# A new instruction order for agent attention with a SiLU MLP, and an empty instruction as token between banks

## Chip, cores and metric

The kernel runs on one NeuronCore of a Trainium2 chip. The metric is the device time of one execution in microseconds (us). TensorE is called PE here (PEld is its weight load), VectorE DVE, ScalarE ACT, GpSimd POOL, and SyncE, which only issues DMAs, SP.

## What is computed

Two batches of 12480 tokens with 128 channels, 49 agents in each batch, then a dense MLP with 2048 hidden units on all 24960 tokens. Inputs are float32 (the two weights are float64).

```python
def _attn_ref(q, k, v, agents):
    scale = 1.0 / np.sqrt(q.shape[-1])
    def sm(a, b):
        s = scale * (a @ b.transpose(0, 2, 1))
        s = s - s.max(-1, keepdims=True)
        e = np.exp(s)
        return e / (e.sum(-1, keepdims=True) + 1e-09)
    agent_v = sm(agents, k) @ v
    return (sm(q, agents) @ agent_v).astype(np.float32)

def _moe_ref(x, w_in, w_out):
    h = x @ w_in
    g = h * (1.0 / (1.0 + np.exp(-h)))
    return (g @ w_out).astype(np.float32)
```

## The kernel before, in words

Tokens go in 13 tiles of 960 per batch, 26 in all. For a batch, all tiles of k and v are folded into the 49 x 128 matrix `agent_v` (running maximum, exponentials, transposes, products); that matrix times `w_in` gives the folded weight A2 of the batch, held as two float16 parts `A2h` and `A2l`. For a q tile the softmax over the agents is made and turned by a DMA into `pT`. The MLP then runs on the tile in 16 steps of 128 hidden units, 416 steps in all.

- **front** (`front`, L610): six matmuls make the hidden block `h` of a step.
- **gate** (`gate`, L622, ACT): SiLU into half of a tile `g`, which holds two steps, a pair.
- **hi half** (`split`, L636 on ACT or L638 on DVE, as the string `HI` says) and **lo half** (L642, DVE) split `g` into the float16 tile `hl` (one of its six buffers bears the name `vx`).
- **back** (`back`, L664): twelve matmuls of a step add into two PSUM banks `o0` and `o1`. The halves of the PE array swap banks in the middle of every four backs. So that the third back of four does not write before the second has ended, the second is followed by a token on POOL (L670), a memset of one element that waits for the last matmuls of the second back; the first matmuls of the third back wait for that memset.
- **out_part** (L687 DVE, L689 ACT) scales a finished tile into an output tile `os`, of which there are two, and **out_store** (L697, SP) stores it.

The q tiles from the third on have a path of their own, two tiles at a time: `q_absmax` (L338, DVE) takes the largest magnitude of each tile into a small tile `mx2`; `q_total` (L342, PE) sums it into a PSUM tile `x`; `q_scales` (L192, L349, L352, DVE) makes from it the scales `sk`, `ik` and two tiles `es`; `split_khl` (L756 ACT, L759 DVE) splits the q tile and frees its load buffer (`kq`, five of them, shared with k); `q_exp` (L569, ACT) uses `es`; `q_norm`, `q_parts` (DVE) and `q_turn` (L588, DMA) make `pT`. The small tiles are rings: two `mx2`, two `sk`, three `ik`, six `es`, so a writer waits for the reader of the tile before last, and so on. PSUM tiles `x` are a ring of two, which a_mm (L542, the product that makes A2) uses too.

No engine chooses its work at run time. Four strings in `PLAN`, one letter per job, fix the order of the jobs on SP, PE (P), ACT (A) and DVE (D); `issue` takes the next letter of each engine when what `job` was given as `deps`, `after` and buffers (`take`, `give`) has been issued, and `in_order` ties every instruction to the one before it on its engine. At run time an instruction waits for what it reads and for the buffer it overwrites, whatever stands in `deps` or `after`; an instruction that waits holds up all that stands behind it on its engine. The strings come from a planner outside the file, which is not shown here.

Of the kernel before, what the change touches and what calls it, by code (L numbers as in the profile page):

```python
# [48 lines left out]
PLAN = {
    "S": (  # L50
        "kakkkqvkawkwkvkkkkkkvvvvwvvqwvvvvvkkkqtkqvvtqqtvkvvkkvkqoovktqvtktokkvqqvootvovkqqqtotqqovqttqqotqqt"
        "qoootqoqtqotqqottottoootttootoototoo"),
    "P": (
        "WkkwkwwwukQwwkwwwwwwwwwwwwkttwwwwwtvktkvkktktkwwwwkvvv1ttww2ttvv3vwwQtwwwwwwwvttvvvvk4ua56aakffafmff"
        "fkbffbfbfbbffbffbfbffbbfbbttbffbfbbffqqfbbffbfbbbffbtkvvmfbffbbfbfbfbfbffbbkvkfbfbffbbffbfbqqfbfbfbf"
        "bffbbbbfbttbffbbffbffbffbftvkkmbfbbffbbffbbbffbvvkffbfbffbbffbbfbbffbqqbfbfbffbbffbbfbfttfbffbbfbfvt"
        "mbfbfbfbkvvkkfbfbbffbffbffbbffbbffbbfbfqqbffbbffbffbkfbfbfbbbbffbbttfbfbtmfbbfbfbffvvvt1ffbbbfbffbfb"
        "fbbfbbffbffbffb2qmbfbb3vfbbffb4qfbfbffbbfbffbbffbbfbfbffbbfbbfbffb6aaffbffbbbfbbffbbffbqqfbfbfbfbfbf"
        "bbfbfbfbbfbbfmaafbfbfbffbbffbffbbbffbffbfbbfbfbbffbfmqffbqmbfbfbfbfbbffbbfqmfbffbfbbfbffbffbbfbfqqbb"
        "bfbfbfbfbfbfbbffbfbbffbfbfbfbfbfbqmfbffbfbbfbfbbqmbffbffbffbbffbbbffbffbbbffbfbfbffbbfbfbqqffbfbfbbf"  # L60
        "fbbffbbffbbffbbffbfbffbbffbfbffbbbfbfbffbqqffbbfbfbfbbfbbffbffbffbbbffbffbfbfbbffbffbbbffbbffbbffbbf"
        "bbffbffbbbffbbbffbfbbfqffbfbfbbbffbffbfbbffbffbbbbffbbffbfbfbffbfbfbffbffbbbffbbbfbffbbffbbfbffbfbbf"
        "bffbfbfbfbffbbbfbbffbbfbffbfbffbfbfbbffbfbfbbbfbbffbffbfbfbffbbffbbffbbffbfbbbfbffbffbbfbbffbfbfbfbb"
        "bfbbbbbb"),
    "A": (
        "xxcectttxxtcxcttxttxfccttetccttskawaakggagggigggiggiggwggghgkgxghggigotggiggggeegikgighggiggiggihokg"
        "gggiggkggggiggggxeggioggggggtggkggegggigkhhggigggoggkgiggiggxggggggeggtgoggeigggiikhgghkggiggggggkig"
        "gogigigggggggiggiggxkeegoggtiggxggigghgigghgggiiggogggggfggegiggiggigghgggoggegggggiggigggagghagoggi"
        "giggiggggeegggiggohgaghggiggaggggiggggiggigogggihgggigghgiggigghggiggggoggieeegghigggghggiggigoggigg"
        "giggiggiggggeeeggggoggigiggghggihggggggiggoiggggiggigggghggigggggogghgggiiggiggggggeeeggogggghggiggg"  # L70
        "gggiggiggggoggggegggiggigiggiggogggggegggggggiggiggoggggggggggiggiggigggoggigggeggggggggiggoggiggggg"
        "ggiggggggoggggggggggggiggggggogggigggggigo"),
    "D": (
        "xr12sxr5xnr1657xr8xprxrdx6dr73845d90d67s5An86d7dd8BCE2FDyamaamGwiajHyjpcijjjijwiylrijjtiljomjsjisjnp"
        "mtdjcjiljjydjnopjliyjdjijiyssjjirjminjptojimjijitdjijyincjjilydjjiopjlydrjijisjjijisjijiomtjmdjtnncp"
        "jdydijyjjijijjoylrpljjijisjsmjjimjyotnrnijijctjdmddpj3ljijtmpjjoijij49sicj0dnlApjijBjsjijiojijiEnijj"
        "jpFmjlijimjolmaajmjssjiGijnjijmjicpojijnjilHjaijjpijlamjojiscjljmjsimjcjjisljjicojlijnpsjnjiijjljspo"
        "jmmjijjmsljjmcijinjiojpnjjijiljcjijlsipjojnpjijjjsijiljjijiojijnjsljjijpijinjoijiijjjijinjsjjijoiiji"
        "pjjlsjnpjjjoijiijjijiijpjnjjiojijijijsijpjjjiojjijijijijnpijjoinjjijijjipjijijoijijijijijjijijoijijj"
        "ijjijo"),  # L80
# [945 lines left out]
```

## Time and profile before

| | us |
|---|---|
| median of three runs | 909.35 |
| lowest and highest run | 905.48, 909.81 |
| the profiled execution's own time | 909.31 |
| its span, first to last instruction | 907.5 |
| PE busy in the span | 873.9 |
| DVE busy, ACT busy | 813.0, 728.4 |

The span leaves out 1.8 us of the execution's time. Matmul ends are modelled, so a busy PE is not always PE at its peak. In the timeline a bracket at a row's end gives how long the engine stood idle before the row and what ended that.

### The profile page before, as it was taken

How to read it: one execution, taken by the hardware profiler on the slowest of the kernel's cores; microseconds unless marked ns; L12 is line 12 of the kernel's file. 1: busy time of each engine (PE TensorE's matmuls, PEld its weight loads, DVE VectorE, ACT ScalarE, POOL GpSimd, SP SyncE). 2: the span in 40 equal slices, each digit the busy share in tenths (PEclk: the TensorE clock that was granted, in tenths of full speed). 3: DMA queues.
4: the chain of work that ended last, by engine and by line, in shares of the span. 5: the costliest groups of instructions: out<-in, count | busy, mean ns of one | idle time of the engine just before them, and what ended most of it. 6: DMA issues, size and time to landing. Idle time of an engine off the chain costs nothing.

```text
span 907.5 us, 20159 instructions
## 1 busy us (share of the span) xinstructions
PE 873.9 (96%) x8879; PEld 443.4 (49%) x8879; DVE 813.0 (90%) x817; ACT 728.4 (80%) x704; POOL 24.5 (3%) x114
## 2 busy tenths in 40 slices
PE   7989999999999999999899799899999999999997
PEld 4645555545554555445345344454544444444443
DVE  4799989999999899998899688999999899799985
ACT  4579997788988989888689779788887977877563
POOL 1000000000000000000000000000000000000000
PEclk9999999999999999999899899999999999999999
DMA  9982074016014023030040112110010101101100
GB/s 346 389 266 56 1 196 134 15 43 186 23 35 144 22 81 87 2 78 2 11 122 23 46 45 67 35 35 13 2 56 23 25 1 56 35 2 35 34 23 22
DMA packets 43410, 63.89 MB, mean 70 GB/s; under 512 B 29475, under 2 KB 29731, under 8 KB 42811
## 3 DMA queue, kind: packets, MB, share of 16 engines
q1 hardware_dynamic: 43323, 62.61, 23.0%
q8 instruction: 69, 1.13, 0.5%
q14 instruction: 18, 0.15, 0.1%
HBM read 43.01 MB, written 12.78 MB: 61 GB/s over the span
## 4 chain that ended last, share of the span: by engine, by line
PE 82%; DVE 6%; ACT 3%; issue 1%; POOL 1%; DMA 1%; SPq 0%; POOLq 0%; DVEq 0%; ACTq 0%
PE o L664 52%; PE h L610 25%; DVE hl L642 3%; PE x L479 1%; DVE hl L638 1%; ACT g L622 1%; PE x L380 1%; POOL token L670 1%; PE x L463 1%; PE x L361 1%; DMA outT<-os 1%; PE x L362 1%; PE x L363 1%; PE x L542 0%; ACT hl L636 0%
## 5 line engine op out<-in xcount | busy, mean ns | idle before, releaser
L622 ACT ACTIVATE g<-h,sA 128x960 f32<-128x960 f32 x416 | 425.0, 1057 | 106.7 <-PE h L610 97.3
L642 DVE SCALAR_TENSOR_TENSOR hl<-g,tS,hl 128x1920 f16<-128x1920 f32 x173 | 380.7, 2213 | 21.5 <-ACT hl L636 19.1
L664 PE MATMUL o<-hl,woh 64*128 64x480 f16 x2768 | 383.9, 365 | 13.0 <-DVE os L687 6.6
L664 PEld LDWEIGHTS <-woh 64*128 64x128 f16 x3328 | 164.7, 94 | 189.8 <-issue 15.8
L610 PE MATMUL h<-pT,A2h 64*128 64x480 f16 x1664 | 238.9, 364 | 0.7 <-ACT g L622 0.6
L664 PE MATMUL o<-hl,wol 64*128 64x480 f16 x1384 | 198.7, 365 | 0.0
L610 PE MATMUL h<-pT,A2l 64*128 64x480 f16 x832 | 153.8, 364 | 0.0
L636 ACT ACTIVATE hl<-g,tS 128x1920 f16<-128x1920 f32 x76 | 143.7, 1894 | 1.4
L610 PEld LDWEIGHTS <-A2h 64*128 64x128 f16 x1664 | 83.0, 94 | 89.2 <-issue 10.7
L638 DVE TENSOR_SCALAR hl<-g,tS 128x1920 f16<-128x1920 f32 x97 | 117.6, 1213 | 9.5 <-ACT g L622 9.4
L664 PEld LDWEIGHTS <-wol 64*128 64x128 f16 x1664 | 83.1, 94 | 86.5 <-issue 1.4
L664 PE MATMUL o<-vx,woh 64*128 64x480 f16 x560 | 79.9, 363 | 1.3 <-DVE os L687 1.3
L642 DVE SCALAR_TENSOR_TENSOR vx<-g,tS,vx 128x1920 f16<-128x1920 f32 x35 | 77.4, 2212 | 1.3 <-PE o L664 0.5
L610 PEld LDWEIGHTS <-A2l 64*128 64x128 f16 x832 | 41.6, 94 | 43.2 <-issue 0.7
L670 POOL MEMSET token<- 1x1 f32 x104 | 21.9, 211 | 875.3 <-PE o L664 868.1
L664 PE MATMUL o<-vx,wol 64*128 64x480 f16 x280 | 39.9, 362 | 0.0
L689 ACT ACTIVATE os<-o,oS 128x480 f32<-128x480 f32 x26 | 17.2, 661 | 23.4 <-PE o L664 21.3
L687 DVE TENSOR_SCALAR os<-o,oS 128x480 f32<-128x480 f32 x26 | 18.6, 715 | 15.1 <-PE o L664 13.3
L338 DVE TENSOR_REDUCE mx<-q 128x1 bf16<-128x960 f32 x24 | 27.4, 1147 | 4.5 <-PE x L342 4.5
L638 DVE TENSOR_SCALAR vx<-g,tS 128x1920 f16<-128x1920 f32 x24 | 29.1, 1213 | 1.3 <-ACT g L622 1.3
L756 ACT ACTIVATE khl<-q,ik 128x960 f16<-128x960 f32 x24 | 26.1, 1090 | 4.8 <-DVE ik L349 4.8
L759 DVE SCALAR_TENSOR_TENSOR khl<-q,ik,khl 128x960 f16<-128x960 f32 x24 | 29.0, 1210 | 0.0
(171 smaller groups left out, 559.8 us busy)
## 6 DMA issues: line engine op xcount, KB each, us to landing
k<-kT SPq DMA_DIRECT2D x26, 480.0 KB, 8.1
q<-qT SPq DMA_DIRECT2D x26, 480.0 KB, 5.1
outT<-os SPq DMA_DIRECT2D x25, 480.0 KB, 3.1
vt<-vP SPq DMA_DIRECT2D x13, 480.0 KB, 7.7
vt<-vP SPq DMA_DIRECT2D x9, 512.0 KB, 8.4
...
```

Of the source, the lines that this page charges most:

```text
L338: V.tensor_reduce(st["mx", n][:, u:u + 1], tiles[key], axis=AX.X, op=ALU.max, apply_absolute_value=True)
L610: T.matmul(ps[:, u, :HT], w[wt][rs, fs], t[rs, x * HB:(x + 1) * HB, 0:CH], start=(n == 0), stop=(n == 2))
L622: A.activation(hid[s // 2][:, s % 2], hps.pop(s)[:, :, :HT], AF.Silu, scale=batch[b]["sA"][:, 0:1])
L636: A.activation(hid[p][1], g, AF.Copy, scale=t)
L638: V.tensor_scalar(hid[p][1], g, t, None, op0=ALU.mult)
L642: V.scalar_tensor_tensor(lo, g, t, hi, op0=ALU.mult, op1=ALU.subtract)
L664: mm = T.matmul(acc[u], wt[rs, j + x, :], g[rs, x, u, :], start=(a and x == 0 and n == 0), stop=(z and x == 1 and n == 2)).ins
L670: acc["told"] = G.memset(token, 0.0).ins
L687: V.tensor_scalar(o[:, 0:HT], last_acc[0], oS, None, op0=ALU.mult)
L689: A.activation(o[:, HT:ST], last_acc[1], AF.Copy, scale=oS)
L756: A.activation(t[:, 0, 0:ST], tiles[key], AF.Copy, scale=st[key, "inv"])
L759: V.scalar_tensor_tensor(l[:, 0:ST], tiles.pop(key), st.pop((key, "inv")), hi[:, 0:ST], op0=ALU.mult, op1=ALU.subtract)
```

## The change

The strings `HI` and all four of `PLAN` are new. In the job table some conditions move from `after` (issued before) to `deps` (a need), which is what the planner reads; for the program itself `issue` treats both alike. The conditions are the reuse of `mx2` (q_total of the pair four q tiles earlier), of `ik` and `es` (lo split and exponentials of six and five q tiles earlier), of the output tiles (the store two tiles earlier) and of the v buffers of batch 1 (each of the first four waits for the one product of batch 0 that read it, where all of them waited for the last). The token is `nop` where it was `memset`, and its tile is gone, so line numbers behind L598 are lower by one.

```diff
 HI = (
-    "DAADADDDDAADAADAAADADDADDADDDDDADADADADDDDDAAADADDAAADDAADDADAADAADDDADAADDDDDAADDAAADDDADDADDADAADA"
+    "DADAAADDDAAADDADAADDDDAAADAADADAAADDDDDAAAADDADDDAAADDDDADAADAADDDDAAADADADDADADDAAADDAADDADAAADADAD"
...
     "S": (
-        "kakkkqvkawkwkvkkkkkkvvvvwvvqwvvvvvkkkqtkqvvtqqtvkvvkkvkqoovktqvtktokkvqqvootvovkqqqtotqqovqttqqotqqt"
+        "kkakkwkkvqvkkkkwkkkvvwvvvvqwvvvvvakkktqqkqvkvtqovvvkktqqkktvkkqvktqovtkvqotovvqotvqqtvqoqtooqqtqoqto"
...
-    token = cp.tile([1, 1], F32, name="token")
...
         if r == 1:
-            acc["told"] = G.memset(token, 0.0).ins
+            acc["told"] = G.nop(nofuse=True).ins
             for mm in mms.values():
                 tc.add_manual_dep(acc["told"], mm.name, SYNC, reason="banks")
...
-            xs_.append(job("D", "m", q_absmax, key, n, u, deps=[l], after=xs_ + ([lows[n - 4][0]] if n - 4 in lows else [])))
+            xs_.append(job("D", "m", q_absmax, key, n, u, deps=[l] + ([lows[n - 4][0]] if n - 4 in lows else []), after=xs_))
         x = job("P", "m", q_total, n, deps=xs_, take=("x",))
-        sc = job("D", "c", q_scales, n, keys, deps=[x] + [ags[key[1]] for key in keys], give=("x",),
-                 after=[lows[n - 6][1], expd[n - 5]] if n - 6 in lows else [])
+        sc = job("D", "c", q_scales, n, keys, deps=[x] + [ags[key[1]] for key in keys] +
+                 ([lows[n - 6][1], expd[n - 5]] if n - 6 in lows else []), give=("x",))
...
-            l = job("S", "v", load, *key, take=("vt",), after=avl[-1:])
+            l = job("S", "v", load, *key, take=("vt",), deps=[avl[(12, 7, 8, 9)[i + u]]] if i + u < NV else [])
...
-            parts_ = [job("DA"[u], "o", out_part, k, u, deps=ready, after=stores[n - 2:n - 1] if n > 1 else [],
+            parts_ = [job("DA"[u], "o", out_part, k, u, deps=ready + (stores[n - 2:n - 1] if n > 1 else []),
```

Three places of the new order follow, each as it was and as it is.

**Place 1, reuse of `es`, batch 1, pairs around step 210 to 218.** ACT before (`L569` are the exponentials that read `es_5694` and `es_5696`; a number in `g` or `h` is the step):

```order
L622 ACTIVATE g214_6559<-h215_6560,sA1_4979 128x960
L689 ACTIVATE os_207_6581<-o1_192_6104,oS0_714 128x480
L622 ACTIVATE g216_6590<-h216_6583,sA1_4979 128x960
L622 ACTIVATE g216_6590<-h217_6591,sA1_4979 128x960
L636 ACTIVATE hl5_893<-g214_6559,tS1_4981 128x1920
L569 ACT_TABLE_LOAD
L569 ACTIVATE D_6156<-D_6156,es_5694 120x392
L569 ACTIVATE D_6288<-D_6288,es_5696 120x392
L569 ACTIVATE D_6462<-D_6462,es_6162 120x392
```

DVE before, where `es_6608` and `es_6610` take the places of `es_5694` and `es_5696`:

```order
L638 TENSOR_SCALAR hl4_892<-g212_6504,tS1_4981 128x1920
L192 TENSOR_SCALAR sk_6604<-x_6435 128x2
L349 RECIPROCAL ik_6606<-sk_6604 128x2
L352 TENSOR_SCALAR es_6608<-sk_6604,ags1_727 128x1
L352 TENSOR_SCALAR es_6610<-sk_6604,ags1_727 128x1
L687 TENSOR_SCALAR os_207_6581<-o0_192_6103,oS0_714 128x480
L642 SCALAR_TENSOR_TENSOR hl4_892<-g212_6504,tS1_4981,hl4_892 128x1920
```

The same on ACT now (the exponentials read `es_4677`, `es_5590` and `es_5592`):

```order
L621 ACTIVATE g216_6627<-h217_6674,sA1_4681 128x960
L569 ACT_TABLE_LOAD
L569 ACTIVATE D_6232<-D_6232,es_4677 120x392
L569 ACTIVATE D_6239<-D_6239,es_5590 120x392
L569 ACTIVATE D_6420<-D_6420,es_5592 120x392
L621 ACT_TABLE_LOAD
L621 ACTIVATE g218_6715<-h218_6708,sA1_4681 128x960
L621 ACTIVATE g218_6715<-h219_6772,sA1_4681 128x960
```

and on DVE now, where `es_6808` takes the place of `es_4677`:

```order
L641 SCALAR_TENSOR_TENSOR vx_112<-g216_6627,tS1_4683,vx_112 128x1920
L637 TENSOR_SCALAR hl1_113<-g218_6715,tS1_4683 128x1920
L192 TENSOR_SCALAR sk_6802<-x_6380 128x2
L349 RECIPROCAL ik_6804<-sk_6802 128x2
L352 TENSOR_SCALAR es_6806<-sk_6802,ags1_726 128x1
L352 TENSOR_SCALAR es_6808<-sk_6802,ags1_726 128x1
L641 SCALAR_TENSOR_TENSOR hl1_113<-g218_6715,tS1_4683,hl1_113 128x1920
```

Before, the DVE wrote `es` ahead of the lo half of pair 212, while the exponentials that it waits for stood behind the gates of pair 216. Now it writes `es` behind the hi half of pair 218, whose gates stand behind those exponentials on ACT.

**Place 2, reuse of `mx2`.** PE before (`x_5679` is q_total of `mx2_5131`, `x_5681` and `x_5702` are the first two a_mm of batch 1):

```order
L610 MATMUL h180_5671<-pT_5138,A2l0_710 128x480
L342 LDWEIGHTS ones12_94
L342 MATMUL x_5679<-mx2_5131,ones12_94 128x2
L542 MATMUL x_5681<-win_114,avT_100 128x512
L542 MATMUL x_5702<-win_114,avT_100 128x512
L610 LDWEIGHTS A2h0_709
```

DVE before, where `mx2_5686` takes the place of `mx2_5131`:

```order
L638 TENSOR_SCALAR hl3_891<-g174_5504,tS0_713 128x1920
L642 SCALAR_TENSOR_TENSOR hl3_891<-g174_5504,tS0_713,hl3_891 128x1920
L338 TENSOR_REDUCE mx2_5686<-q_1_5_5282 128x1
L642 SCALAR_TENSOR_TENSOR hl4_892<-g176_5568,tS0_713,hl4_892 128x1920
L638 TENSOR_SCALAR hl5_893<-g178_5611,tS0_713 128x1920
L192 TENSOR_SCALAR sk_5690<-x_5679 128x2
```

The same tile of q on DVE now, where `mx2_5168` takes the place of `mx2_3810`:

```order
L637 TENSOR_SCALAR hl2_835<-g160_5118,tS0_712 128x1920
L641 SCALAR_TENSOR_TENSOR hl1_113<-g158_5086,tS0_712,hl1_113 128x1920
L338 TENSOR_REDUCE mx2_5168<-q_1_5_5034 128x1
L551 SCALAR_TENSOR_TENSOR A2l1_4680<-x_4816,iA1_4682,A2h1_4679 128x512
L641 SCALAR_TENSOR_TENSOR hl2_835<-g160_5118,tS0_712,hl2_835 128x1920
```

and q_total of `mx2_3810` on PE now:

```order
L363 MATMUL x_4592<-agh0_255,khl1_106 128x49
L342 LDWEIGHTS ones12_94
L342 MATMUL x_4626<-mx2_3810,ones12_94 128x2
L609 LDWEIGHTS A2h0_708
L609 MATMUL h138_4628<-pT_3690,A2h0_708 128x480
```

Before, the reader stood on PE behind front 180, and the DVE wanted the tile just behind the lo half of pair 174. Now the reader stands ahead of front 138, and the DVE wants the tile behind the hi half of pair 160, which needs front 161.

**Place 3, the load queue ahead of the store of tile 9 (`os_159`).** SP before (`q_1_7` takes the load buffer that the split of `q_1_2` frees; on DVE that split stands four rows ahead of the write of `os_191`, which takes the place of `os_159`):

```order
L234 DMA q_1_6_5828<-qT 128x960
L588 DMA_TRANSPOSE pT_5830<-phl0_98 128x8x128
L234 DMA q_1_7_5956<-qT 128x960
L697 DMA outT<-os_159_5273 128x960
L697 DMA outT<-os_175_5684 128x960
```

and now (`q_1_6` takes the buffer that the split of `q_1_1` frees, on DVE 60 rows ahead of the write of `os_191`):

```order
L696 DMA outT<-os_143_4935 128x960
L234 DMA q_1_6_5371<-qT 128x960
L588 DMA_TRANSPOSE pT_5373<-phl1_99 128x8x128
L696 DMA outT<-os_159_5353 128x960
L588 DMA_TRANSPOSE pT_5817<-phl0_98 128x8x128
```

The store now stands behind a load that is freed much earlier.

## Rows read from the trace of the kernel before

**Rows 1.** The page: engines, busy us, share; then the chain that ended last.

```profile
PE 873.9 (96%) x8879; PEld 443.4 (49%) x8879; DVE 813.0 (90%) x817; ACT 728.4 (80%) x704; POOL 24.5 (3%) x114
...
PE 82%; DVE 6%; ACT 3%; issue 1%; POOL 1%; DMA 1%; SPq 0%; POOLq 0%; DVEq 0%; ACTq 0%
```

**Rows 2.** Stretches: length, then busy us of PE, PEld, DVE, ACT, POOL; clock; DMA.

```profile
0.00:60.00 60.00, 50.27 (x483) 32.99 (x485) 42.93 (x102) 30.36 (x52) 2.58 (x10) 1.00 0.99 366
...
100.00:425.00 325.00, 324.77 (x3375) 165.98 (x3373) 305.80 (x319) 287.07 (x276) 8.98 (x39) 1.00 0.27 73
425.00:575.00 150.00, 135.22 (x1372) 65.94 (x1370) 127.67 (x127) 117.68 (x107) 2.46 (x17) 0.94 0.17 48
```

**Rows 3.** Timeline at 431 to 436: start, us, engine, line, work, count [idle before].

```profile
431.18 0.18 PE L342 MATMUL x<-mx,ones 128*128 128x2 bf16 x1
...
431.22 1.10 PE L542 MATMUL x<-win,avT 128*128 128x512 f32 x2
431.40 1.16 DVE L338 TENSOR_REDUCE mx<-q 128x1 bf16<-128x960 f32 x1 [4.51 <-PE x L342]
...
435.93 2.07 PE L542 MATMUL x<-win,avT 128*128 128x512 f32 x2 [3.60 <-DVE sk L192]
```

**Rows 4.** Chain that ended last, before and after that wait: start, us, what.

```profile
427.61 0.61 PE h L610 x6
428.21 2.43 PE o L664 x24
...
438.00 1.31 PE h L610 x6
439.32 2.08 PE o L664 x12
```

**Rows 5.** Timeline of DVE, ACT and PE at 509 to 512, then the chain there.

```profile
510.14 0.21 DVE L352 TENSOR_SCALAR es<-sk,ags 128x1 f32<-128x1 f32 x1 [6.37 <-ACT D L569]
...
509.49 1.65 ACT L569 ACTIVATE D<-D,es 120x392 f32<-120x392 f32 x3
...
511.55 0.98 PE L664 MATMUL o<-hl,woh 64*128 64x480 f16 x4 [6.62 <-DVE os L687]
...
511.55 4.80 PE o L664 x24
```

**Rows 6.** Timeline of PE at 568 to 571, then the chain behind it.

```profile
568.79 0.58 PE L664 MATMUL o<-hl,woh 64*128 64x480 f16 x4 [1.33 <-DVE hl L638]
571.05 0.98 PE L664 MATMUL o<-hl,woh 64*128 64x480 f16 x4 [1.26 <-DVE hl L642]
...
572.03 2.28 PE h L610 x12
```

**Rows 7.** Timeline of DVE and PE at 464 to 471.

```profile
463.98 1.21 DVE L759 SCALAR_TENSOR_TENSOR khl<-q,ik,khl 128x960 f16<-128x960 f32 x1
...
470.52 0.72 DVE L687 TENSOR_SCALAR os<-o,oS 128x480 f32<-128x480 f32 x1 [1.49 <-DMA outT<-os]
...
471.29 0.58 PE L664 MATMUL o<-vx,woh 64*128 64x480 f16 x4 [1.34 <-DVE os L687]
```

**Rows 8.** PE's waits for the token; the token's durations; tokens over 150 ns; one place.

```profile
PE o L664 <- POOL token L670: 3.4, 7, 0.7
...
L670 POOL MEMSET token<- x104: 88/88/1130, 71.1 to 900.3; 1x1 f32 x104
...
147.15 1.13 POOL L670 MEMSET token<- 1x1 f32 x1 [7.81 <-PE o L664]
...
872.55 0.86 POOL L670 MEMSET token<- 1x1 f32 x1 [6.59 <-PE o L664]
...
531.05 1.22 DVE L638 TENSOR_SCALAR hl<-g,tS 128x1920 f16<-128x1920 f32 x1 [2.42 <-ACT g L622]
531.25 1.04 POOL L670 MEMSET token<- 1x1 f32 x1 [7.20 <-PE o L664]
...
532.36 0.58 PE L664 MATMUL o<-hl,woh 64*128 64x480 f16 x4 [0.62 <-POOL token L670]
```

More of the change, by code (lines that the diff above doesn't have):

```diff
@@ L45 @@
 HI = (
-    "DAADADDDDAADAADAAADADDADDADDDDDADADADADDDDDAAADADDAAADDAADDADAADAADDDADAADDDDDAADDAAADDDADDADDADAADA"
-    "ADAADADADADDAAADAAADDDAADDADDAADAADDADDDAAADDDDDDADDAADDDDAAAADDDDDDAADDDDDAAADADDDDDADADDADDDDDDDDA"
-    "DDDDADAD")
+    "DADAAADDDAAADDADAADDDDAAADAADADAAADDDDDAAAADDADDDAAADDDDADAADAADDDDAAADADADDADADDAAADDAADDADAAADADAD"
+    "ADADADDADDDAAADADADAAADDADDDDDDADDADAADAADADDDDDDDAADDADADAADDDDADDDDDDDDDADDDDDADDAADDAADDDDDADADAD"
+    "AADDADDD")
 PLAN = {
     "S": (
-        "kakkkqvkawkwkvkkkkkkvvvvwvvqwvvvvvkkkqtkqvvtqqtvkvvkkvkqoovktqvtktokkvqqvootvovkqqqtotqqovqttqqotqqt"
-        "qoootqoqtqotqqottottoootttootoototoo"),
+        "kkakkwkkvqvkkkkwkkkvvwvvvvqwvvvvvakkktqqkqvkvtqovvvkktqqkktvkkqvktqovtkvqotovvqotvqqtvqoqtooqqtqoqto"
+        "tqqqtoqtootqoqtototttooottotooottooo"),
@@ L53 @@
     "P": (
[L54 to L63, printed above, removed]
@@ L64 @@
-        "bfbbbbbb"),
-    "A": (
[L66 to L72, printed above, removed]
@@ L73 @@
-    "D": (
[L74 to L80, printed above, removed]
+        "WwwwwwwwwwwkkwwwwwwwwukkwwwkttkvQwwktkkwkvtwwwwwktktkvvwww1ttwt2vvv3vtQtwwwwwvtvvtvvww4ku5w6aaafaffk"
@@ new lines @@
+        "fffkmfbfbffbbfbfbfbbfbfbffbfbfbfbttbfqqbffvkfbfbmtbfbbfbfvkvkffbbbffbffbfbfbbfbffbfqqfbbkbttbmtfbffb"
+        "ffbbffbbffbbfbbffbfbffkvvkvqqffbbffbfbfbfbffbbbfbfbbfbfbfbbffbffbfbbbfttbfbffbfbbffbbmkvktffbbffvvkk"
+        "qffbffbffbbfbbffbfbfbfbbbfbfbbffbfbbftqfbfbfbtmfbbbfbffbffbfbfbbbbfbfbfftvvvt1fbfbfbffbfbfbfbf2qmfbb"
+        "b3vbfbfbfbfbfbffbbfbfbb4qmfbfbfbfbfbffbf6aaffbfbbfbffbffbbfbfbfbfbffbffbbbffbbbfbffbbqqffbfbfbbbbffb"
+        "ffbfbfmaabfbffbfbfbfbbffbqmfbffbbfbfbffbbbffbfbffbbbfbffbqqfbfbffbbfbfqmbfbfbffbbfbbfbbffbffbfqfbbfb"
@@ new lines @@
+        "bbbffbffbfbbffbbffbfbfbbfqmffbbfbbfbffbfbbfbmqfbffbbbffbfbbffbfbfbffbbbffbfbffbffbfbbfbbfbfbffbbffbb"
+        "fbfbffbbqqfbffbffbfbbfbfbfbffbfbfbbffbfbfbfbffbfbfbbbfbfbbffbfbfbbffbffbffbbbfbfbfbfbbfbfbfqqfbbffbf"
+        "bfbfbfbffbbbffbbffbbfbbffbffbfbffbbbffbbfbfbfbfbfbfbffbffbffbbfbbffbfbfbfbbffbffbbqffbbffbfbffbbfbff"
+        "bbbfbfbbbffbffbbfbfbbffbbffbbfbfbfbffbfbffbffbbffbfbfbbffbbfbbfbfbffbbfbfbffbfbfbbfbbffbfbfbbbfbffbf"
+        "fbbbfbbbbbb"),
+    "A": (
+        "xtccxtxexttxtcctxtxctfcttetccttskawaagaggkggigggigkgwggiiggghgghgxggtgigogikgiggeeghkgghgiggkggiggig"
+        "gogggxkteegggggighgigggigghgikggkioggggigggggeiggigiggoggggxeggggggtiggikhgkghiggkiggggoggiggggxeggg"
+        "kgigggioggigxegggggtgggigggghoiggiggggiggghgfieggggggoggiggiggigghgggigagggaigggoggigghggggiggeggigg"
+        "ioghggiggeeggggiggaigaggggigogghgiggiggggighgggiggigogghgiggghgiggggiegghggggogigeeeggggggiggiggiggo"
+        "ggghiggggihgggiggiggigoghggggigggggggggeegggoggiggggggigggggigigggoggiggigggigghggeegghggogggggggggi"
+        "gigggegggoigghggiggggiggigggggogggggggiggggggggggggoggeggggiggggggegggggoggigggeggiggiggggoggiggiggg"
+        "gggggggggiggogggigggigggggigiggoggggiggggggo"),
@@ new lines @@
+    "D": (
+        "xr152xrxr678sxrxr5nxrxr6d7358d4d9p6d07As5n86d7d1d8BCE2FDyGamaHamaijwjiyjcyjpwjjijirjlitljssojdmmjcji"
+        "ytjdnlpiyjjiyrjdjnjlopssiimmtjjcyijijjnjltjipjdydldyrojjijsjnisjnmjjjoijiipjpjmitjijjcdynpytjddlyjji"
+        "orjijjsijmijinyrjjlmmotjsjipjmijicjmijnjijtdoddtljpjijj34s9mcljijijd0iojiAjjBjncEpjsijFljimjjiojiajj"
+        "ijmlijijmajnGjojlspsjimjijncjjiajijaojijpHlnjscjijjplmijmjojsiljsijjsijjjlijiojnjpmijicjlijjsmjjonip"
+        "jljicmjsmjinjjjpnojijijsjijijpiijjlciojijljiijjjsnpijjjiojnjjijjipjiljiljoijijijisjnjnjipjipojjsijnj"
+        "ijpjjijijosijijijjijiljijijiojijijijjijinijjijopijsjiijnjjnpjijoijjjijijijijipjojijjijjijjjoijijjiji"
+        "jijo"),
@@ L922, in agent_attention_then_silu_mlp @@
             kept.append(x)
-            x = job("P", "v", lambda key: av_products(key, psum(C)), key, deps=[l, x], take=("x",), give=("vt", "eT"))
+            x = job("P", "v", lambda key: av_products(key, psum(C)), key, deps=[l, x], take=("x",), give=(("vt", l), ("eT", x)))
             y = job("D", "d", av_add, key, g, u == 0, deps=[x] + ([y] if y else [avend]), give=("x",))
@@ L946, in agent_attention_then_silu_mlp @@
             e = HI[p]
-            x = job(e, "i", split, p, 0, A if e == "A" else V, deps=gates[-2:] + [unit1[b]] + ([avl[NST - 1]] if p == 0 else []),
-                    after=his_[-1:] + ([ws[w, h] for w in ("in", "out") for h in range(NW)] if p == 2 else []), take=("hl",))
+            x = job(e, "i", split, p, 0, A if e == "A" else V, deps=gates[-2:] + [unit1[b]] + ([avl[NST - 2]] if p == 0 else []) +
+                    ([ws[w, h] for w in ("in", "out") for h in range(NW)] if p == 2 else []), after=his_[-1:], take=("hl",))
             his_.append(x)
```

## Prediction

> **What bounds the kernel now.** I read the page first. PE is busy 96% of the span, and the chain that ended last lies 82% on PE [rows 1]. DVE, at 90%, is close behind and is the engine on which a misplaced instruction hurts. Only less matmul work or fewer holes on PE can shorten such a kernel. The change keeps the matmuls: counted by letters, both orders have 416 fronts, 416 backs, 26 jobs each for scores of k, turns and products, 24 of q; only the warming matmuls grow, by six. So the question is where PE stands idle or slow.
>
> The second view cuts the span into stretches [rows 2]. From 100 to 425 us PE is busy 324.77 of 325 us: there is nothing to win there, and it shows that the order's plan of durations is good. From 425 to 575 us PE is busy 135.22 of 150 us, at a granted clock of 0.94. In the first 60 us it is busy 50.27 us, while the DMA engines are full (share 0.99, 366 GB/s). The holes are thus in the start and in one piece of 150 us in the middle.
>
> The third view is the timeline and the chain in that piece: four places, each a wait for a buffer that is overwritten.
>
> 1. *mx2.* At 431.40 the DVE has stood 4.51 us, until q_total (L342) on PE has read the small tile that absmax (L338) overwrites [rows 3]. Behind it on DVE stand a lo half, a hi half, then the scales that free the PSUM tile for the second a_mm; PE waits 3.60 us for it.
> 2. *es.* At 510.14 the DVE has stood 6.37 us until ACT has done the exponentials that read the old `es`; behind it stand the output write and the lo half of pair 212. PE waits 6.62 us [rows 5].
> 3. *es again.* At 568 PE waits 1.33 and then 1.26 us for the halves behind another such write [rows 6].
> 4. *os.* The store of tile 9 stands on SP behind a load that waits for the split at 463.98; the output write waits 1.49 us for that store, PE 1.34 us [rows 7].
>
> Idle is not the whole price. Behind the first wait a front takes 1.31 us where it took 0.61 before it, and twelve matmuls of a back 2.08 us, where 24 took 2.43 [rows 4]; that is the lower of the two clock levels (1.2 against 2.4 GHz), granted after PE had stood idle.
>
> **The change, part by part, against the profiled execution's own 909.31 us** (the median is 909.35, so nothing is to be shifted).
>
> *mx2 wait goes.* Idle 3.60. Slow matmuls: the a_mm pair 2.07 - 1.10 = 0.97 [rows 3], the front 1.31 - 0.61 = 0.70, the back 2.08 - 2.43/2 = 0.86 [rows 4]. Sum 6.1 us. In the new order (place 2) the reader stands ahead of front 138, the writer behind a hi half that needs front 161: 23 fronts later on PE, so the tile has been read whenever the DVE gets there. What is late next is nothing: the DVE then waits for the front, as in the stretch without holes.
>
> *First es wait goes.* Idle 6.62, and 24 matmuls in 4.80 us against 2.43: 2.37 [rows 5, 4]. Sum 9.0 us. Place 1 shows why it can't come back there: the hi half of pair 218 on DVE needs gates that stand on ACT behind the exponentials, so the write of `es` behind that half finds them done.
>
> *Second es wait goes.* 1.33 + 1.26 idle, and twelve matmuls of two fronts in 2.28 us against 2 x 0.61: 1.06 [rows 6, 4]. Sum 3.65 us.
>
> *os wait goes.* 1.34 us [rows 7]. In place 3 the store of tile 9 now stands behind a load whose buffer is freed 60 DVE rows ahead of the write that needs the store, where it was four.
>
> *Token.* Of 104 memsets 21 took over 150 ns (the first 1.13 us at 147.15, the last 0.86 us at 872.55), the median 88 ns; PE waited 3.4 us in 7 of them [rows 8]. At 531 the memset starts 0.20 us after a DVE hi half (L638) and ends with it, 532.29 against 532.27; each of the 21 ends so with an L638. The trace before has no empty instruction. Its bounds: no gain if it is held as the memset was, 3.4 us if it never is. I take 3.4, since it writes nothing that a DVE instruction could hold; even at 88 ns it would be hidden behind the front that stands between second and third back in nearly all cases. The Trainium skill ("SBUF — State Buffer", section "SBUF: two separate sides") says that VectorE and GpSimd share a port pair as an exclusive lock, so that one of the two blocks fully. By that rule an instruction without an SBUF operand is never held and the term is the full 3.4 us; without it, by the rows alone, the term could be 0 and the sum 889.2. This trace agrees for the memsets; no run here shows the empty instruction.
>
> *Start: 0.* The loads are issued in another order, but up to the last v load of batch 0 both orders hold the same 13 k, 13 v, 4 weight and 2 q loads, on full DMA engines, and the first front needs that last v. The agents of batch 1 go from the ninth load to the place right behind the last v; the DVE reads them ahead of the last sum for `agent_v`, but they are small and issued next to a tile of 480 KB that the same chain awaits. Bounds: two loads of 480 KB later at 366 GB/s is +2.6 us; filling all of PE's idle 60.00 - 50.27 is -9.7 us. I take 0, nearer to the first. The six warming matmuls lie in this idle time.
>
> *Hi halves.* Two of 208 go from DVE to ACT. ACT is busy 80%, so PE covers it; if it didn't, it would show as a PE wait for ACT.
>
> Sum: 909.31 - 6.1 - 9.0 - 3.65 - 1.34 - 3.4 = **885.8 us**.
>
> **Rivals.**
>
> *A new wait takes the place of the old ones.* The strings are new throughout, and DVE has only 325 - 305.8 = 19 us to spare in 325 [rows 2], so one instruction placed some us too early reaches PE, as the four did. For it: the old strings had four such places in 150 us. Against it: all four were buffers whose reuse the old job table gave as order alone, and the new one gives as a need; elsewhere the old strings had next to no holes. Price: one hole as large as the largest seen, 9.0 us: 894.8.
>
> *The start moves.* Another order of loads may let PE fill its idle time: half of 9.7 us gives 881, all of it 876. For it: PE and DVE both have holes there. Against it: the DMA engines are full and the last v bounds it.
>
> *The strings don't do what they say.* Nothing in the program's own waits has changed; were the four waits only moved, the sum would be the token's term alone, 906 to 909. The rows of places 1 to 3 speak against it.
>
> *Slower, by the token.* 104 times PE waits for a signal that goes through POOL. If the empty instruction takes longer than a memset does, every third back is late. With one front in between, a token of 1.04 us left PE idle 0.62 us [rows 8], so the cover is 0.42 us. In the new order 59 third backs have just one front in between (51 before). From 0.42 + 23.5/59 = 0.82 us on, the gain is gone; at the longest memset's 1.13 us the 59 cost 42 us: 928. Only the length of the slowest memsets speaks for it, and those are the held ones; the 88 ns speak against it.
>
> **How the numbers follow.** The forecast, 880 to 892, has 0.72. A new large hole has 0.14 (892 to 902). A start that gains over 6 us has 0.07 (below 880). Waits only moved: 0.04. Slower by the token: 0.03. The range leaves out most of the last three and the far end of the second, some 0.17 in all: 879.5 to 897. A measurement of this kernel tells about 0.5% from no change, 4.5 us; all of the first three cases are faster by more, 0.93; same 0.04, slower 0.03.
>
> **What would show it.** In the new profile: no DVE row of L338 or L352 with an idle of some us ended by PE or ACT, and no output write that waits for a DMA; a granted clock of 1.00 in every stretch of 425 to 575; PE's waits in the middle below 2 us together; tokens that never outlast 0.1 us, and no PE wait on POOL. The prediction is wrong if PE shows a new wait of over 4 us anywhere behind 100 us, if the first front (L610) starts over 3 us away from where it did, at 60 us (where the first stretch of [rows 2] ends), or if the backs wait for POOL.

## The result and the profile after

The changed kernel takes 880.71 us, median of four runs (880.28 to 881.33), against 908.36 (905.48 to 909.81) for the kernel before: a ratio of 0.97, 95% interval 0.9673 to 0.9727. The prediction was 885.8 us, its range 879.5 to 897. Direction and mechanism hold. The time is 5.1 us below the forecast; counted from the medians beside it, 27.7 us were won where the sum gave 23.5, 4.2 more, and 2.6 of that is a term that the sum had at zero, the start. The profiled execution took 880.8 us, its span is 878.7.

The page of the profile after, the lines of [rows 1]: busy us, share and instructions of each engine, then the chain that ended last.

```profile
PE 866.4 (99%) x8885; PEld 439.7 (50%) x8885; DVE 811.2 (92%) x815; ACT 730.1 (83%) x704; POOL 2.6 (0%) x10
...
PE 94%; DMA 2%; DVE 2%; ACT 1%; issue 0%; SPq 0%; ACTq 0%; POOLq 0%
```

PE's share of the chain went from 82% to 94%, DVE's from 6% to 2%. The stretches of [rows 2], with 60 to 100 us between them:

```profile
0.00:60.00 60.00, 53.10 (x497) 35.21 (x499) 44.06 (x105) 32.08 (x54) 2.57 (x10) 1.00 0.98 362
60.00:100.00 40.00, 39.33 (x407) 19.24 (x402) 39.04 (x38) 39.66 (x39) 0.00 (x0) 1.00 0.26 70
100.00:425.00 325.00, 325.00 (x3359) 164.69 (x3359) 308.10 (x326) 289.84 (x277) 0.00 (x0) 1.00 0.27 75
425.00:575.00 150.00, 149.97 (x1602) 74.01 (x1598) 145.66 (x138) 133.33 (x120) 0.00 (x0) 1.00 0.18 48
```

From 425 to 575 us PE is busy 149.97 of 150 us where it was 135.22, at a granted clock of 1.00 where it was 0.94. The first 60 us hold 53.10 us of PE work where they held 50.27, and that was not foreseen.

The groups of instructions by line, 100 to 700 us, for the three writes that waited on the reuse of a buffer: line, engine, operation, count, then busy us, mean ns of one, and the idle time of the engine just before them with what ended it. First before:

```profile
L338 DVE TENSOR_REDUCE mx<-q 128x1 bf16<-128x960 f32 x21 | 24.0, 1147 | 4.5 <-PE x L342 4.5
L687 DVE TENSOR_SCALAR os<-o,oS 128x480 f32<-128x480 f32 x18 | 12.9, 715 | 8.0 <-PE o L664 6.3 <-DMA outT<-os 1.5
L352 DVE TENSOR_SCALAR es<-sk,ags 128x1 f32<-128x1 f32 x22 | 3.7, 201 | 10.2 <-ACT D L569 10.2
```

and after:

```profile
L338 DVE TENSOR_REDUCE mx<-q 128x1 bf16<-128x960 f32 x22 | 25.0, 1147 | 0.0
L686 DVE TENSOR_SCALAR os<-o,oS 128x480 f32<-128x480 f32 x18 | 12.9, 714 | 1.7 <-PE o L663 1.5
L352 DVE TENSOR_SCALAR es<-sk,ags 128x1 f32<-128x1 f32 x22 | 3.5, 199 | 0.0
```

The instructions and their durations are the same; the idle time that PE's q_total (4.5 us), ACT's exponentials (10.2 us) and the store (1.5 us) ended is gone. What is left before `os` is the wait for the finished tile itself, which belongs to the work.

All waits of PE behind 62 us in the profile after (total us, times, longest):

```profile
PE h L609 <- ACT g L621: 0.6, 1, 0.6
PE o L663 <- DVE hl L641: 0.2, 1, 0.2
```

No wait on POOL stands here, where [rows 8] had 3.4 us in seven.

### The profile page after: what moved, and what is told of

It is laid out like the page before. It is cut to its first block, busy times and chain, and to the rows that moved or that the text cites. A ratio compares the mean times of both kernels' runs of the same rounds, so it can differ in the third digit from the quotient of the medians.

```text
span 878.7 us, 20055 instructions
## 1 busy us (share of the span) xinstructions
PE 866.4 (99%) x8885; PEld 439.7 (50%) x8885; DVE 811.2 (92%) x815; ACT 730.1 (83%) x704; POOL 2.6 (0%) x10
## 3 DMA queue, kind: packets, MB, share of 16 engines
q8 instruction: 69, 1.13, 0.5%
## 4 chain that ended last, share of the span: by engine, by line
PE 94%; DMA 2%; DVE 2%; ACT 1%; issue 0%; SPq 0%; ACTq 0%; POOLq 0%
PE o L663 57%; PE h L609 29%; DMA k<-kT 2%; PE x L479 1%; PE x L463 1%; PE x L380 1%; PE x L361 1%; PE h_ps L380 1%; ACT g L621 1%; PE x L363 1%; PE x L362 1%; PE x L542 1%; PE o_ps L479 0%; ACT A2h L547 0%; DVE wo L280 0%
## 5 line engine op out<-in xcount | busy, mean ns | idle before, releaser
L637 DVE TENSOR_SCALAR hl<-g,tS 128x1920 f16<-128x1920 f32 x97 | 117.6, 1214 | 5.8 <-ACT g L621 5.8
L637 DVE TENSOR_SCALAR vx<-g,tS 128x1920 f16<-128x1920 f32 x22 | 26.7, 1213 | 0.0
L635 ACT ACTIVATE vx<-g,tS 128x1920 f16<-128x1920 f32 x13 | 24.6, 1895 | 0.2
## 6 DMA issues: line engine op xcount, KB each, us to landing
vx<-vP SPq DMA_DIRECT2D x4, 512.0 KB, 10.2
```

The source lines that it names most:

```text
L635: A.activation(hid[p][1], g, AF.Copy, scale=t)
L637: V.tensor_scalar(hid[p][1], g, t, None, op0=ALU.mult)
```

## The experiments

The theory was: four reuse waits cost 20 us, the held token 3.4, and nothing else moved. The rivals: only the new order as a whole explains it, or the holes hang together, or the rest lies in the start. Beside each group of runs the kernel before was run on the same chip; its medians were 907.46 (larger rings, empty token alone, old token, old loads), 908.4 (the rings one by one, everything but the order, larger rings in the new order), 908.6 (24 empty instructions, third raw buffer, k first) and 907.6 (the last run).

### Larger rings in the old order

```diff
-            st["mx", n] = sp.tile([P, 2], BF16, tag="mx2", name="mx2", bufs=2)
+            st["mx", n] = sp.tile([P, 2], BF16, tag="mx2", name="mx2", bufs=6)
...
-        inv = sp.tile([P, 2], F32, tag="ik", name="ik", bufs=3)
+        inv = sp.tile([P, 2], F32, tag="ik", name="ik", bufs=8)
...
-            es = sp.tile([P, 1], F32, tag="es", name="es", bufs=6)
+            es = sp.tile([P, 1], F32, tag="es", name="es", bufs=16)
...
-            outs[k] = sp.tile([P, ST], F32, tag="o", name=f"os_{k}"), {0, 1}
+            outs[k] = sp.tile([P, ST], F32, tag="o", name=f"os_{k}", bufs=3), {0, 1}
```

> The order of before, but with more buffers for what is overwritten: mx2 6 (were 2), es 16 (6), ik 8 (3), output tiles 3 (2). Theory: the four holes between 425 and 575 us are waits for these buffers, so they go without any new order, with their slow-clock matmuls: 909.3 - 20.1 = 889.2 us, 886 to 892; the token's waits and the start (first front at 60.0) stay. Rival: DVE is simply too full in that piece of the old order, and the holes come back at another instruction: over 900 us.

Measured: 887.61 us (886.63 to 887.99), ratio 0.977 (0.9751 to 0.9788): 19.85 us won with not one instruction moved. The stretch of the four holes:

```profile
425.00:575.00 150.00, 149.38 (x1580) 75.75 (x1578) 146.77 (x148) 136.34 (x126) 2.73 (x20) 1.00 0.19 53
```

and the largest of PE's waits behind 62 us:

```profile
PE o L664 <- POOL token L670: 3.2, 6, 0.7
```

What follows: the holes were waits for the reuse of these buffers. More buffers remove them as well as another order does.

### The rings one by one

The first of these has only `mx2` enlarged, the second only `es`.

```diff
-            st["mx", n] = sp.tile([P, 2], BF16, tag="mx2", name="mx2", bufs=2)
+            st["mx", n] = sp.tile([P, 2], BF16, tag="mx2", name="mx2", bufs=6)
```

> The old order with six mx2 buffers in place of two, nothing else. Theory (each hole has its own price, read from its own rows): the wait at 431 us goes and the other three stay; 6.1 us off the 907.5 of the kernel before, so 901.4, within 1 us; PE idle 3.60 at the a_mm of batch 1 is gone, PE still waits some 6.6 us and 2.6 us for the es writes. Rival (the holes hang together: what is won at one is waited for at the next): under 3 us gained, 904.5 or more, and the es wait grows by what the first gave.

```diff
-            es = sp.tile([P, 1], F32, tag="es", name="es", bufs=6)
+            es = sp.tile([P, 1], F32, tag="es", name="es", bufs=16)
```

> The old order with sixteen es and eight ik buffers in place of six and three, nothing else. Theory (own prices): both es waits go, 9.0 + 3.65 = 12.65 us off 907.5, so 894.9, within 1.5 us; the 3.60 us idle of PE at the a_mm of batch 1 and the 1.3 us at the output write stay. Rival (the holes hang together): the sum of this run and of the one with more mx2 buffers falls short of the 18.6 us that all rings but the output's should give by over 3 us. Rival 2 (the clock, not the wait, is the price): the gain is that of the idle alone, 6.62 + 2.59 = 9.2 us, so 898.3.

The kernel that ran has sixteen `es` but still three `ik`; the eight `ik` of the expectation are not in it.

Measured: 901.94 us (901.46 to 902.57), ratio 0.9927 (0.9908 to 0.9945), so 6.5 us won; and 895.26 (894.49 to 896.84), ratio 0.9856 (0.9839 to 0.9874), 13.1 us won. With more `mx2`, the stretch from 425 to 575 us:

```profile
425.00:575.00 150.00, 138.71 (x1432) 69.04 (x1430) 132.59 (x133) 122.82 (x113) 2.56 (x18) 0.97 0.19 51
```

and the largest of PE's waits behind 62 us:

```profile
PE o L664 <- DVE os L687: 8.1, 2, 6.6
PE o L664 <- POOL token L670: 3.4, 7, 0.7
PE o L664 <- DVE hl L642: 1.5, 2, 1.3
PE o L664 <- DVE hl L638: 1.3, 1, 1.3
```

The same two views with more `es`, the stretch:

```profile
425.00:575.00 150.00, 144.32 (x1510) 71.35 (x1506) 139.86 (x140) 129.48 (x119) 2.65 (x19) 0.99 0.19 53
```

and the waits:

```profile
PE x L542 <- DVE sk L192: 3.6, 1, 3.6
PE o L664 <- POOL token L670: 3.4, 7, 0.7
PE o L664 <- DVE os L687: 1.5, 1, 1.5
```

In each run exactly the waits of its own ring are gone and the others keep their length, to 0.1 us. Both es waits are gone with three `ik`, so the ring that made them is `es` alone. Singles and whole agree: 6.5 + 13.1 = 19.6 of 19.85, each good to some 1.7 us. Within that the holes are independent. The second rival of the `es` run, the gain of the idle time alone, falls: 13.1 us were won where PE had stood idle 9.2. The granted clock of the stretch rises with each hole removed, 0.94 in [rows 2], then 0.97 and 0.99 here, so the slow matmuls behind a wait are part of its price. The output ring was not run alone; the 0.25 us that are left for it and for `ik` are smaller than the intervals.

### The empty token alone, and the old token in the new order

```diff
-            acc["told"] = G.memset(token, 0.0).ins
+            acc["told"] = G.nop(nofuse=True).ins
```

> The order of before with the empty instruction as token, nothing else. Theory: only PE's shown waits for the token go, 3.4 us: 905.9 us, with the four holes of the middle as they were. Rival 1: an empty instruction signals no sooner than a memset: 909.3, with token waits as before. Rival 2: tokens that outlast their cover cost PE more than its waits show (the pace between 100 and 425 us slips too): 903 to 905.

The old order with this line: 903.15 us (902.74 to 905.06), ratio 0.9947 (0.9926 to 0.9967), 4.3 us won. PE's waits behind 62 us:

```profile
PE o L663 <- DVE os L686: 8.0, 2, 6.6
PE x L542 <- DVE sk L192: 3.6, 1, 3.6
```

The four holes are as they were, the waits for POOL gone. The time lies in the second rival's range, 903 to 905, but theory and rival were counted from 909.3: from the 907.46 measured beside this run, 3.4 us less would be 904.1, and the interval of the gain, 3.0 to 6.7 us, holds both. The better pace between 100 and 425 us that this rival names is not seen: PE is busy 324.85 us of the 325 where it was 324.77.

> The new order with the memset of before as token. Theory: about 20 of 104 memsets fall beside a hi half on DVE and are held, PE waits for some: 880.7 + 3.4 = 884.1 us, 883 to 886. Rival: the token's price depends on the order, and the new order hides it: 880.7 to 881.5, with held memsets but no PE waits.

The changed kernel with the line the other way round: 884.07 us (883.78 to 885.86), ratio 0.9739 (0.9716 to 0.9762), 3.4 us above the changed kernel. The waits are back:

```profile
PE o L664 <- POOL token L670: 2.6, 6, 0.6
```

and so are the long memsets (shortest, median and longest in ns):

```profile
L670 POOL MEMSET token<- x104: 88/88/1061, 69.1 to 874.6; 1x1 f32 x104
```

What follows: the empty token is worth 3.4 us in the new order and 4.3 in the old, and it is not the order that frees it.

### 24 empty instructions as token

```diff
-            acc["told"] = G.nop(nofuse=True).ins
-            for mm in mms.values():
-                tc.add_manual_dep(acc["told"], mm.name, SYNC, reason="banks")
+            first = G.nop(nofuse=True).ins
+            for mm in mms.values():
+                tc.add_manual_dep(first, mm.name, SYNC, reason="banks")
+            for _ in range(23):
+                acc["told"] = G.nop(nofuse=True).ins
```

> The changed kernel with 24 empty instructions in a row as token in place of one. It prices the rival 'slower, by the token' (with one front in between the cover is 0.42 us, 59 third backs have just one). The length p of one empty instruction is not in the trace, so the times go by it. Theory (cover 0.42 us, all 59 pay what lies above it): at p = 0.03 us the token is 0.72 us long and costs 59 x 0.30 = 18 us, 898; at p = 0.06 us 1.44 us long, 59 x 1.02 = 60 us and some us more where two fronts stand in between, 940 or above. Rival (empty instructions run in almost no time, p under 0.018 us): 881. Rival 2 (PE has far more cover than 0.42 us, since weight loads and the second half of the array go on): a token wait in the trace that is at most half of what the lengths give.

Measured: 881.47 us (880.59 to 881.85), ratio 0.9705 (0.9684 to 0.9726), 0.8 us above the changed kernel, which is about the spread of either. Beside the two waits of the profile after, PE shows one more:

```profile
PE o L663 <- POOLq L673: 0.2, 1, 0.2
```

POOLq is POOL's sequencer. It has rows for the first empty instruction of each token (L669) and for the last (L673), and none for those in between:

```profile
L669 POOLq EVENT_SEMAPHORE  x104: 17/17/17, 69.4 to 871.3; - x104
...
L673 POOLq EVENT_SEMAPHORE  x104: 17/17/17, 69.5 to 871.4; - x104
```

The time is that of the first rival. The two rows of the first token start 0.05 us apart, at 69.44 and 69.49, which speaks for a token far shorter than the cover of 0.42 us rather than for the second rival, more cover than that. The length p of one empty instruction can't be read. By the expectation's formula, 59 places times (24 p - 0.42) must stay below some 1 us, so p would be at most about 0.02 us, provided that all 24 are carried out, which no row shows. The rival "slower, by the token" is thus far from this kernel: 24 of them, as written, leave PE one wait of 0.2 us.

### Everything but the order

The old order with all larger rings and the empty token, both edits as above; the conditions in the job table stay as before too.

> The old order with all rings larger and the empty token: everything of the change but the new order itself. Theory (holes, token and start are three separate terms): 907.5 - 19.9 - 3.4 to 4.3 = 883.3 to 884.2; first front near 59 to 60 us, so the rest to the changed kernel's 880.7 is the start. Rival (the new order is better than that in the middle too): 886 or more, with PE's waits between 100 us and the end above 2 us together. Rival 2 (start is worth nothing, rings and token explain all): 881 or below.

Measured: 883.33 us (882.8 to 883.85), ratio 0.9723 (0.9708 to 0.9738). Its stretches:

```profile
0.00:60.00 60.00, 51.19 (x487) 33.62 (x489) 43.52 (x102) 30.86 (x53) 2.57 (x10) 1.00 1.00 368
60.00:100.00 40.00, 38.63 (x393) 19.83 (x389) 39.31 (x39) 38.62 (x39) 0.00 (x0) 1.00 0.21 48
100.00:425.00 325.00, 324.83 (x3369) 166.72 (x3367) 306.50 (x319) 287.86 (x275) 0.00 (x0) 1.00 0.27 73
425.00:575.00 150.00, 150.00 (x1588) 76.28 (x1584) 147.47 (x149) 137.12 (x126) 0.00 (x0) 1.00 0.20 53
```

Within the theory's bounds. The changed kernel is 2.6 us faster than this. PE's idle time, length less busy time, tells where: 8.81 against 6.90 us up to 60, 1.37 against 0.67 from 60 to 100, 0.17 against 0 from 100 to 425, next to nothing in both from 425 to 575. So the new order as such is worth 2.6 us, and all of that lies ahead of 100 us. Two rows and a wait show most of it. The first front here:

```profile
59.48 0.58 PE L609 MATMUL h<-pT,A2h 64*128 64x480 f16 x4
```

in the changed kernel:

```profile
57.69 0.58 PE L609 MATMUL h<-pT,A2h 64*128 64x480 f16 x4
```

and a wait of PE that this run has and the changed kernel has not; it ends at 89.53:

```profile
PE x L463 <- ACT S_ring L433: 0.7, 1, 0.7
```

The first front comes 1.8 us earlier and the wait of 0.7 is gone. Over all profiles the first front starts at 59.06 to 59.97 in the six of the old order, and at 57.19 to 57.69 in the four of the new order with its own start, so the 1.8 us are more than what one profile differs from the next.

### Larger rings in the new order

> The changed kernel with the same larger rings. Theory (no wait for the reuse of a small tile is left in the new order): 880.7, within 0.7 us. Rival (reuse still costs something in the new order that hides in short waits): 2 us or more faster, 878.7 or less.

Measured: 880.65 us (880.09 to 880.88), ratio 0.9693 (0.9678 to 0.9707). No difference: in the new order no reuse of these buffers costs anything. No version tried beats this or the changed kernel.

### The old order of the loads in the new order

The first 34 letters of the string `S` as they were before; PE, ACT and DVE as in the changed kernel.

```diff
-"kkakkwkkvqvkkkkwkkkvvwvvvvqwvvvvva
+"kakkkqvkawkwkvkkkkkkvvvvwvvqwvvvvv
```

> The new order, but the first 34 loads on SP in the order of before. The new kernel's first front starts at 57.7 us, before it did at 60.0, which was not forecast. Theory now: the order of the loads did that: the first front is back at 59.5 to 60.5, and the time at 883 to 884.5 us. Rival: the order of the jobs on DVE, ACT and PE in the start did it: first front at 57.7, 880 to 881.5 us.

Measured: 883.81 us (882.06 to 884.33), ratio 0.9726 (0.9706 to 0.9746), 3.1 us above the changed kernel. With the old loads the start's gain is gone. The same bytes are moved, so why? The chain that ended last, start, us and what, in the changed kernel, from the last wait for a tile of k:

```profile
19.51 7.69 DMA k<-kT
...
27.33 1.03 PE h_ps L380 x4
...
30.48 0.96 PE h_ps L380 x4
```

and with the old loads:

```profile
14.30 11.55 DMA k<-kT
...
25.99 1.03 PE h_ps L380 x4
...
33.24 0.96 PE h_ps L380 x4
```

Three of the 13 score products of k are left behind the last wait in the one, five in the other, so the last one starts at 30.48 against 33.24. But the old order of the loads does not make this by itself. The kernel before has the same 34 loads in the same order, and there the last maximum of the scores of k, which DVE takes behind the last of these products, starts earlier:

```profile
32.56 0.66 DVE L389 TENSOR_REDUCE gm<-h_ps 128x1 f32<-128x480 f32 x1
```

In the six profiles of the old order it starts at 31.73 to 32.56, in the changed kernel at 31.48, here at 34.24. So most of what this run loses comes from the old loads under the new order of the jobs on PE, ACT and DVE. The run shows that the new jobs need their own loads; the new loads under the old jobs were not run, so how the start's gain divides between loads and jobs is not shown.

At the same time a queue stall shows: with the old loads the DMA engines' share from 40 to 45 us falls to 0.66, while the last weight load waits on SP until 40.90 for a raw buffer, one of the two into which the weights are loaded before they are converted. Two candidate causes, late products and the stall, which the next run tells apart.

### The old loads with a third raw buffer

```diff
-NR = 2
+NR = 3
```

> The changed kernel with the old order of the first 34 loads, as in the run before that gave 883.8, and three raw buffers in place of two. Theory (the old order loses by the queue that stalls: the last weight load waits on SP for a raw buffer until 40.9 us, behind it stand the last v loads, and the DMA engines run dry): with a third buffer the stall goes, the DMA engines stay at a share near 1.0 from 40 to 45 us where it was 0.66, the first front comes 2 to 3 us earlier than 60.66 and the time is 881 to 882. Rival (the last k loads come later in the old order, and that sets the end whatever the queue does): 883.3 or more, first front at 60 us or later.

Measured: 882.88 us (882.77 to 883.18), ratio 0.9723 (0.9703 to 0.9743): 0.9 us of the 3.1 came back, which is less than the intervals (the two ratios differ by 0.0003). The stretch from 40 to 45 us, with two raw buffers:

```profile
40.00:45.00 5.00, 4.63 (x64) 3.76 (x60) 4.40 (x14) 3.15 (x6) 0.00 (x0) 1.00 0.66 222
```

and with three:

```profile
40.00:45.00 5.00, 4.64 (x61) 3.78 (x57) 4.40 (x14) 2.95 (x5) 0.00 (x0) 1.00 1.01 410
```

The DMA engines are full again, and yet the first front starts at 60.13, as the rival had it (60 or later); the time lies between the two, nearer to the rival's 883.3. That dry DMA engines cost the start its 3 us falls. What the start hangs on in the new order of the jobs is shown by two DVE rows of each run: the last maximum of the scores of k (L389, 128 x 480) and the first hi half (L637). In the changed kernel:

```profile
31.48 0.66 DVE L389 TENSOR_REDUCE gm<-h_ps 128x1 f32<-128x480 f32 x1 [0.19 <-PE h_ps L380]
...
62.14 1.21 DVE L637 TENSOR_SCALAR vx<-g,tS 128x1920 f16<-128x1920 f32 x1
```

with the old loads:

```profile
34.24 0.66 DVE L389 TENSOR_REDUCE gm<-h_ps 128x1 f32<-128x480 f32 x1 [0.19 <-PE h_ps L380]
...
64.84 1.21 DVE L637 TENSOR_SCALAR vx<-g,tS 128x1920 f16<-128x1920 f32 x1
```

and with the third raw buffer as well:

```profile
33.75 0.66 DVE L389 TENSOR_REDUCE gm<-h_ps 128x1 f32<-128x480 f32 x1 [0.19 <-PE h_ps L380]
...
64.12 1.21 DVE L637 TENSOR_SCALAR vx<-g,tS 128x1920 f16<-128x1920 f32 x1
```

The distance is 30.66, 30.60 and 30.37 us, and DVE is busy 28.1, 28.1 and 28.0 of it: conversion of the weights, sums for `agent_v`, q softmax, scales, all in a fixed order. From the first hi half to the end of the span it is 816.6, 816.5 and 816.6 us. So in these runs the whole later kernel is moved by what moves the last maximum of the k scores. That DVE's work makes the 30.6 us is argued from its busy time; PE is busy nearly as long there, 28.1, 27.8 and 27.4 us. The next run bears on that.

### One weight piece behind the last k loads

```diff
-"kkakkwkkvqvkkkkwkkkvvwvvvvqwvvvvva
+"kkakkwkkvqvkkkkkkkwvvwvvvvqwvvvvva
```

> The changed kernel with the fourth weight piece behind the last three k loads of batch 0 instead of ahead of them, nothing else. Theory (the first front hangs on the last k tile, which landed at 27.2 us after 7.7 us in full DMA engines): one piece of weight of 1 MB at some 410 GB/s less ahead of it lands it up to 2.6 us earlier, and if nothing else comes up the first front moves from 57.7 to 55.1 to 57 and the time to 878 to 880. Rival (DVE, busy 4.9 of 5 us from 45 to 55 us with the weights' conversion, sets the end, or waits for the later weight): 880.7 or more.

Measured: 883.97 us (882.75 to 884.82), ratio 0.9731 (0.9705 to 0.9757): 3.3 us lost where 0.7 to 2.7 were to be won. The rival had it, by its second half. DVE in this run:

```profile
31.18 0.69 DVE L252 TENSOR_SCALAR cvf<-raw_in 128x1024 uint32<-128x1024 uint32 x1 [4.96 <-DMA raw_in<-w_in]
```

On DVE the conversion of that piece stands ahead of the last maxima. It waits 4.96 us for the later weight, and the last maximum comes at 35.35 instead of 31.48; no wait for PE or k stands ahead of it any more. The first hi half follows at 65.79, 30.44 us behind, and the end 816.6 us behind that. A miss, but the same distance; and PE is busy only 25.7 us in it, DVE 28.1 as before, which speaks for DVE as what makes its length. (What the expectation calls the fourth weight piece is the second, the last of w_in.)

### The first front ahead of w_out

```diff
 P
-4ku5w6aaafaffk
+4w6aaf5akuaffk
 A
-skawaagagg
+saagakwagg
 D
-86d7d1d8BCE2FDyGamaHama
+86d7ddBEFGa8CDa1Hya2mma
```

(Pieces of the three strings; the rest of each is as it was.)

> The changed kernel with the same jobs in another order between the last sum for agent_v and the second front: the sign of the last w_out piece (L280), the scale of w_out and the agents of batch 1 come behind the first piece of A2 instead of ahead of it, on DVE, PE and ACT alike. It asks which work on DVE sets the end of the start. In all the runs so far the first front started 26.2 to 26.4 us behind the start of the last maximum of the k scores (L389, 31.48 in the changed kernel), on a DVE that had next to no idle time in between. Theory (what stands ahead of the first front on DVE sets it): 1.2 us of DVE work leaves that stretch, the first front starts 0.8 to 1.4 us earlier than 57.69, and the time is 879.3 to 879.9. Rival (DVE's whole work up to the first splits sets it, in whatever order): the first front is earlier, but the first hi half on DVE (62.14) and the time are where they were, 880.2 to 881.2. Rival 2 (the first back, 66.25, waits for the later w_out): 881.5 or more.

Measured: 884.65 us (883.82 to 885.36), ratio 0.9742 (0.9725 to 0.9759). The first front did come earlier, at 56.36 instead of 57.69, as the theory said; and the kernel lost 3.9 us. Neither the theory's time nor the first rival's holds; the second rival's bound does. (The 26.2 to 26.4 us from the last maximum to the first front, which the expectation gives for all runs, hold for the new order alone; in the six profiles of the old order they are 26.8 to 27.5.) The rows of DVE and PE:

```profile
55.79 0.75 DVE L551 SCALAR_TENSOR_TENSOR A2l<-x,iA,A2h 128x512 f16<-128x512 f32 x1 [1.14 <-ACT A2h L547]
...
60.52 0.65 DVE L389 TENSOR_REDUCE gm<-S_ring 128x1 f32<-128x480 f32 x1 [1.30 <-ACT S_ring L386]
...
65.45 1.21 DVE L637 TENSOR_SCALAR vx<-g,tS 128x1920 f16<-128x1920 f32 x1
...
70.17 0.84 PE L663 MATMUL o<-vx,wol 64*128 64x480 f16 x4 [1.73 <-DVE wol L306]
```

The last maximum was in time (31.01), but the stretch to the first hi half grew to 34.44 us with the same work in it (DVE busy 28.57): the jobs that were moved ahead wait for ACT and PE, 1.14 and 1.30 us are two of these waits, and DVE stood idle where it had been covered by w_out's conversion. The hi half comes 3.3 us late, `wol` too, PE waits 1.73 us for it, and its next groups of four matmuls take 0.84 to 1.01 us where 0.57 is usual; the granted clock from 70 to 75 us is 0.66, and 0.96 from 60 to 100.

## Why the prediction was right, and where not

**The bound.** That PE was the bound with holes in one piece of 150 us, and that the end moves by what the holes hold, is shown: `mx2` and `es`, each taken away by itself, gave their own price.

**mx2**, 6.1 us: measured 6.5. **Both es waits**, 12.65: measured 13.1. Idle time plus the slow matmuls right behind it was the right price, and a little low: matmuls beyond the few counted were slow too. The clock of 1.00 in the stretch after says the same. **os**, 1.34: not measured apart; the rings leave 0.25 us for it, within some 1.7.

**Token**, 3.4: measured 4.3 in the old order and 3.4 in the new, so right, and the upper bound of the two was the one to take. Of the seven waits, six (3.16 us) stand behind a memset that was held; the last, 0.27 us at 900.41, stands behind one of 88 ns, and it is gone with the empty token too. The Trainium skill ("SBUF — State Buffer", section "SBUF: two separate sides") says that VectorE and GpSimd contend only for the port pair that they share. The prediction drew from it that an instruction without an SBUF operand is never held; the runs agree, since with the same DVE work no wait of PE's matmuls for the token is left.

**Start**, 0 within -9.7 to +2.6: this is the step that failed. It was said that both orders move the same loads "on full DMA engines" and that "the first front needs that last v". The DMA engines are full, at 0.98, but the last v does not set the time of the first front. In the changed kernel its load is issued at 40.91 and has landed 9.9 us later, at 50.8, and its product starts at 51.23; in the kernel before it has landed at 51.1, and its product starts at 52.63. PE waits 1.1 us for v in the whole start (0.6, 0.3 and 0.2), and from the last maximum of the k scores DVE has 28 us of work in 30.7, with no idle time in it that a load of v ended. What the order changed, with equal rings and token, is 2.6 us. The last maximum starts 0.9 us earlier (32.37, now 31.48). In the old order PE then stands idle 0.94 us ahead of 55.34, on DVE, and has a product of k (L380, 1.03 us) at 58.52, right ahead of the first front; in the new order that product stands at 53.41, ahead of the products that wait for DVE. These two agree with the 1.8 us by which the first front comes earlier. Another 0.7 are the wait for `S_ring` that ended at 89.53. How much of the earlier maximum belongs to the loads and how much to the jobs stays open. The bounds held the term; the value that I took was chosen nearer to the wrong one of them, and that the time still fell inside the range owes something to the width of it: 880.71 is 1.2 us above its lower end, and the first front came 2.3 us earlier, where 3 was the sign of being wrong.

**Hi halves**, 0: nothing in the profile after speaks against it; no wait of PE for ACT beyond the 0.6 us is there. It was not tried alone.

**The rivals.** No new wait took the place of the old ones: PE's two waits behind 62 us are 0.8 us together. "The start moves" was the right place at a smaller size, 2.6 us where it took 4.9 or 9.7. "The strings do not do what they say" falls with the rows by line. "Slower, by the token" is met by 24 empty instructions at no measurable cost.

The sum with measured terms: 6.5 + 13.1 + 4.3 + 2.6 = 26.5 of the 27.7 us between 908.36 and 880.71; the rest, 1.2, is within the uncertainty of the medians and holds what the output ring may be worth.
